# A routed mixture of experts: blocks by rank of count, shared weights, and pairs of small experts

## The chip, the cores and the metric

The kernel runs on one core of a Trainium2 chip. The metric is device time in microseconds. The core's engines are TensorE (PE in the rows, its weight loads PEld), VectorE (DVE), ScalarE (ACT), GpSimd (POOL) and SyncE (SP), which issues most transfers. Each has its own queue and works it in order.

## The reference

Top-k attention, a dense mixture, and a routed mixture of eight experts, one after the other. The change lies in the last.

```python
def _moe_ref(x, w_in, w_out, alpha):          # 2304 tokens, 512 wide, hidden 2048
    h = x @ w_in
    g = np.maximum(h, 0.0) + alpha * np.minimum(h, 0.0)
    return g @ w_out

def _moe2_ref(x, w_skip, w_gate, w1, w2):     # 8 experts, hidden 1024
    do_compute = x @ w_skip > 0
    out = x.copy()
    xc = x[do_compute]
    logits = xc @ w_gate
    e_idx = np.argmax(logits, axis=1)
    ...                                       # gate_w: softmax probability of e_idx
    for e in range(E):
        mask = e_idx == e
        h = np.maximum(xc[mask] @ w1[e], 0.0)
        y[mask] = gate_w[mask, None] * (h @ w2[e])
    out[do_compute] = xc + y
```

All values are 32-bit floats.

## The kernel before

Attention runs batch by batch (four of them), and the dense first mixture of one half batch runs between the attention steps of the next. `main` orders all of it: attention steps stand in a table, other work in queues (`todo`, `rowq`, `late`) that `slot` empties by a budget. The last half batch (320 tokens) has no attention beside it: after `main` a loop calls `slot` until the queues are empty. There `up` (L624) and `down` (L670) stream the first mixture's weights through three tiles `wr`, a megabyte each.

Then `rows` routes each half batch. `logits` (L736) gives gate and skip scores, `row` transposes the tokens and stores them (L755, L765), `route` and `rest` choose an expert on VectorE, `ranks` (L815, L816) counts the tokens of each expert by two products, and `slots` gives each token a place in its expert's list. `scatter` (L839) writes an entry per token (its row in the scratch `x2d`, its row in the output, its weight) into the table `tbl` in DRAM, by an indirect transfer that GpSimd issues. `cnt` holds the counts so far.

The second mixture works by blocks of 128 tokens of one expert. A block fetches its entries and its rows of x by indirect transfers (`xgather`, L1012), transposes and splits them (`xsplit`, L1020 to L1022), multiplies by w1 (`first`, L1030), transposes and splits the hidden rows (`hsplit`, L1038 to L1040), multiplies by w2 (`second`, L1048), adds and scatters (`finish`, L1056, L1059). TensorE multiplies in a fast 32-bit format of fewer bits; to keep the precision, each operand is split into a high part (ScalarE's copy) and a low part (VectorE's difference), and each product is made of three: high by high, low by high, high by low. Weights are split as well: one expert's w1 or w2 comes in four tiles of 128x1024 (`wraw`, L995), and `wsplit` splits each (L1001 on ScalarE, L1002 on VectorE). So `first` and `second` are 24 products of 512 columns each.

There are eleven blocks: one early block, one block per expert, and two extra ones. After three of four batches `pick` chooses the expert with most tokens so far; its first 128 tokens are the early block, whose entries and rows are fetched while the first mixture still runs. Its weights are fetched and split from the 38th `slot` of the last loop on (`TL0`, `TL1`), and then again for its second block. `extras` finds on chip the two experts that get the extra blocks. Each block loads and splits its own weights, so there are 88 tiles. `order_` lists them, `loads` and `splits` work the list. What the eleven blocks do not hold, a loop behind them does (`blocks`), one block per turn, only if the count on chip says so.

Of the kernel before, what the change touches and what calls it, by code (L numbers as in the profile page):

```python
# [18 lines left out]
NX = 2  # L19
# [22 lines left out]
ES = 3  # L42
G1 = 12
G2 = 33
RB = 8
# [4 lines left out]
TL0 = 38  # L50
TL1 = 8
TS = 0.6
TG = 6
# [5 lines left out]
def kernel(  # L59
# [132 lines left out]
    sel = const.tile([128, E], F32, name="sel")  # L192
    nc.vector.memset(sel, 0.0)
    est = const.tile([128, 1], F32, name="est")
    nc.vector.memset(est, -1.0)
# [13 lines left out]
    def defaults():  # L209
        nrd = E * RE // 128 + 1  # L210
        dflt = moe.tile([128, nrd, 4], F32, name="dflt", tag="g", bufs=8)
        nc.gpsimd.memset(dflt, 0.0)
        nc.gpsimd.memset(dflt[:, :, 1:2], 4096.0)
        return nc.sync.dma_start(tbl[0:128 * nrd, :].rearrange("(p r) c -> p r c", p=128), dflt)
# [508 lines left out]
    def rows(b, us, colof, x2t, hook, then):  # L723
# [69 lines left out]
        def rest():  # L793
# [4 lines left out]
            for i, u in enumerate(us):  # L798
                base, step = (b * S + u, SF) if u < SF else (b * S + SB, 1)
                v.tensor_scalar(row[:, i, 1:2], pcol, float(step), float(base), op0=OP.mult, op1=OP.add)  # L800
            v.tensor_scalar(c[:, 1], c[:, 1], 1e-9, None, op0=OP.add)
            v.tensor_scalar(c[:, 6], c[:, 3], -1.0, 1.0, op0=OP.mult, op1=OP.add)
            v.tensor_scalar(c[:, 5], row[:, :, 1], float(E * RE + 128), None, op0=OP.add)
            v.tensor_scalar(row[:, :, 0], row[:, :, 1], float(ZR), None, op0=OP.add)
# [42 lines left out]

        parts = [(lambda: not early[0] and rroom(), None), (0.1, logits)] + [(0, None)] * RD
# [11 lines left out]
    outs, wx = [], []  # L860
    NB = 1 + E + NX

    def wtile(half, odd, ch):
        if odd:
            return mr.tile([128, 2, 1024], F32R, name="w2h", tag="w2h", bufs=8)
        if not half:
            return ml.tile([128, 2, 1024], F32R, name="w1h", tag="w1h", bufs=4)

        if ch % 2 == 0:
            if not wx or ch:  # L870
                wx[:] = [xtile(ch // 2).rearrange("p a n s -> p (a n s)")]
            x = wx[0]
        else:
            x = wx.pop()
        c0 = ch % 2 * 2048
        return x[:, c0:c0 + 2048].rearrange("p (a c) -> p a c", a=2)

    early_ = {}

    def pick():  # L880


        v = nc.vector
        w = const.tile([128, 2, E], F32, name="pw")
        c = const.tile([128, 3], F32, name="pc")
        v.tensor_reduce(c[:, 0:1], cnt, axis=AX.X, op=OP.max)
        v.tensor_scalar(w[:, 0], cnt, c[:, 0:1], None, op0=OP.is_ge)
        v.tensor_tensor(w[:, 0], w[:, 0], e8, op=OP.mult)
        v.tensor_reduce(c[:, 1:2], w[:, 0], axis=AX.X, op=OP.max)
        v.tensor_scalar(sel, e8, c[:, 1:2], None, op0=OP.is_equal)  # L890
        v.tensor_scalar(est, c[:, 1:2], -1.0, float(E), op0=OP.mult, op1=OP.add)
        v.tensor_scalar(c[:, 2:3], est, float(RE), pcol, op0=OP.mult, op1=OP.add)
        v.tensor_scalar(w[:, 1], sel, 128.0, None, op0=OP.mult)
        v.tensor_tensor(cnt, cnt, w[:, 1], op=OP.max)
        ri = const.tile([128, 2], I32, name="pri")
        v.tensor_copy(ri[:, 0:1], c[:, 2:3])
        v.tensor_copy(ri[:, 1:2], est)
        experts[0] = nc.values_load(ri[0:1, 1:2], engines=[mybir.EngineType.SP], min_val=0, max_val=E - 1,
                                    skip_runtime_bounds_check_because="an expert by its making")
        early_["ri"] = ri  # L900

    def early_entries():
        t4 = const.tile([128, 4], F32, name="pt4")
        nc.gpsimd.indirect_dma_start(out=t4, out_offset=None, in_=tbl[0:E * RE + 128, :],
                                     in_offset=bass.IndirectOffsetOnAxis(ap=early_["ri"][:, 0:1], axis=0))
        early_["t4"] = t4

    def early_rows():
        ids = const.tile([128, 2], I32, name="pids")
        nc.vector.tensor_copy(ids, early_["t4"][:, 0:2])  # L910
        early_["ids"] = ids
        x = xtile(0).rearrange("p a n s -> p (a n s)")
        wx[:] = [x]
        early_["xg"] = x[:, 4096:4608].bitcast(F32)
        xgather(ids, early_["xg"])

    def first_rows():


        ta = ml.tile([128, 2, E, 4], F32, name="ta", tag="ta", bufs=1)  # L920
        for h in range(2):
            nc.sync.dma_start(ta[:, h], tbl[0:E * RE, :].rearrange("(e n) c -> n e c", n=RE)[h * 128:(h + 1) * 128])
        return ta

    def first_ids(ta):
        v = nc.vector
        s_ = sel[:, :, None].to_broadcast([128, E, 4])
        v.tensor_tensor(ta[:, 1], ta[:, 1], s_, op=OP.mult)
        ns = ml.tile([128, E], F32, name="ns", tag="ns", bufs=1)
        v.tensor_scalar(ns, sel, -1.0, 1.0, op0=OP.mult, op1=OP.add)  # L930
        v.tensor_tensor(ta[:, 0], ta[:, 0], ns[:, :, None].to_broadcast([128, E, 4]), op=OP.mult)
        v.tensor_tensor(ta[:, 0], ta[:, 0], ta[:, 1], op=OP.add)
        ids = ml.tile([128, E, 2], I32, name="idsa", tag="idsa", bufs=1)
        v.tensor_copy(ids, ta[:, 0, :, 0:2])
        return [(ta[:, 0, e], ids[:, e]) for e in range(E)]

    def count():

        gtj = ml.tile([128, E, 18], F32, name="gtj", tag="gtj", bufs=1)
        nc.vector.tensor_tensor(gtj, j128[:, None, :].to_broadcast([128, E, 18]),  # L940
                                cnt[:, :, None].to_broadcast([128, E, 18]), op=OP.is_lt)
        nx = ml.tile([128, E], F32, name="nx", tag="nx", bufs=1)
        nc.vector.tensor_reduce(nx, gtj, axis=AX.X, op=OP.add)
        nc.vector.tensor_tensor(nx, nx, sel, op=OP.subtract)
        nc.vector.tensor_scalar(nx, nx, 0.0, None, op0=OP.max)
# [4 lines left out]
    def extras(kk, n, skip=1):  # L950

        v = nc.vector
        z = ml.tile([128, 2, NX, E], F32, name="z", tag="z", bufs=1)[:, :, 0:n]
        c = ml.tile([128, 4, NX], F32, name="zc", tag="zc", bufs=1)[:, :, 0:n]
        cb = cum[:, None, :].to_broadcast([128, n, E])
        v.tensor_tensor(z[:, 0], cb, kk[:, :, None].to_broadcast([128, n, E]), op=OP.is_le)
        v.tensor_reduce(c[:, 0], z[:, 0], axis=AX.X, op=OP.add)
        v.tensor_tensor(z[:, 1], z[:, 0], cb, op=OP.mult)
        v.tensor_reduce(c[:, 1], z[:, 1], axis=AX.X, op=OP.max)
        v.tensor_tensor(c[:, 1], kk, c[:, 1], op=OP.subtract)  # L960

        v.tensor_scalar(c[:, 1], c[:, 1], 128.0, 128.0 * skip, op0=OP.mult, op1=OP.add)
        v.tensor_scalar(c[:, 2], c[:, 0], est, 128.0, op0=OP.is_equal, op1=OP.mult)
        v.tensor_tensor(c[:, 1], c[:, 1], c[:, 2], op=OP.add)
        v.tensor_scalar(c[:, 2], c[:, 0], float(E) - 0.5, None, op0=OP.is_lt)
        v.tensor_tensor(c[:, 1], c[:, 1], c[:, 2], op=OP.mult)
        v.tensor_scalar(c[:, 3], c[:, 0], float(RE), pcol, op0=OP.mult, op1=OP.add)
        v.tensor_tensor(c[:, 3], c[:, 3], c[:, 1], op=OP.add)
        ri = ml.tile([128, 2, NX], I32, name="ri", tag="ri", bufs=1)
        v.tensor_copy(ri[:, 0, 0:n], c[:, 3])  # L970
        v.tensor_scalar(ri[:, 1, 0:n], c[:, 0], float(E - 1), None, op0=OP.min)
        return ri

    def extra_rows(ri, k):
        t4 = ml.tile([128, 4], F32, name="t4", tag="t4", bufs=NX)
        nc.gpsimd.indirect_dma_start(out=t4, out_offset=None, in_=tbl[0:E * RE + 128, :],
                                     in_offset=bass.IndirectOffsetOnAxis(ap=ri[:, 0, k:k + 1], axis=0))
        return t4

    def extra_ids(t4):  # L980
        ids = ml.tile([128, 2], I32, name="ids", tag="ids", bufs=NX)
        nc.vector.tensor_copy(ids, t4[:, 0:2])
        return ids

    def expert(ri, k):
        return nc.values_load(ri[0:1, 1, k:k + 1], engines=[mybir.EngineType.SP], min_val=0, max_val=E - 1,
                              skip_runtime_bounds_check_because="at most E - 1 by the minimum taken")

    def wfetch(e, half, ch):

        src, nk = ((w1f, KD), (w2f, KE))[half]
        raw = ml.tile([128, 1024], F32, name="wraw", tag="wraw", bufs=RB)
# [4 lines left out]
        return raw  # L997

    def wsplit(half, odd, ch, raw, eng=None):
        hl = wtile(half, odd, ch)  # L1000
        nc.scalar.activation(hl[:, 0], raw, AF.Copy)  # L1001
        nc.vector.tensor_tensor(hl[:, 1], raw, hl[:, 0].bitcast(F32), op=OP.subtract)  # L1002
        return hl
# [499 lines left out]
```

## Time and profile before

| | us |
|---|---|
| median of three runs (lowest, highest) | 1060.57 (1058.77, 1061.43) |
| the profiled execution | 1059.77 |
| its span | 1058.0 |
| TensorE busy in the span | 922.0 (87%) |
| VectorE busy | 903.6 (85%) |
| ScalarE busy | 685.3 (65%) |
| GpSimd busy | 372.4 (35%) |
| bytes moved | 249.94 MB, 236 GB/s in the mean |

The shares are means over stages with different limits: attention with the first mixture beside it until about 820 us, the first mixture's last half batch alone until 888, and the second mixture from there. What an edit is worth is read from its stage. In the rows, `us` behind a start is the time from the first instruction's start to the last one's end in a merged row; a bracket says how long the engine had been idle and which work ended that. A product of full 32-bit floats appears as two records, of the fast format as one.

### The profile page before, as it was taken

What the parts mean: (1) busy time and instruction counts of PE and PEld (TensorE: products, weight loads), DVE (VectorE), ACT (ScalarE), POOL (GpSimd) and SP (SyncE); (2) the same over time, 40 slices, a digit from 0 to 9 for tenths busy, and PEclk for the clock granted to TensorE, in tenths of its full rate; (3) what the DMA queues carried; (4) which work ended last, traced back from release to release, by engine and by line L of the source; (5) the groups of instructions that cost most, each with busy time, mean ns of one, the idle gap of its engine ahead of it and who ended that gap; (6) DMA issues with size and microseconds to landing.
All of it is one profiled execution on the core that took longest, in us unless ns stands there. A gap on an engine that the chain in (4) does not pass through costs nothing.

```text
span 1058.0 us, 21752 instructions
## 1 busy us (share of the span) xinstructions
PE 922.0 (87%) x7206; PEld 834.9 (79%) x7206; DVE 903.6 (85%) x2943; ACT 685.3 (65%) x1740; POOL 372.4 (35%) x529
## 2 busy tenths in 40 slices
PE   4446578999999989999988999998889898898995
PEld 2334468898999879899988998998889897687884
DVE  5999999998998999899979998998993334798972
ACT  7879867666765776576557667756663443596860
POOL 5865643323421342253123323401421421336220
PEclk9967689998999999999989999999999998899998
DMA  8979886576565667766556777665557898899960
GB/s 239 338 249 255 273 264 216 191 243 188 190 223 205 195 195 236 249 206 221 186 162 218 230 234 239 207 218 174 178 186 269 258 377 325 279 354 398 344 223 16
DMA packets 137387, 249.94 MB, mean 236 GB/s; under 512 B 61166, under 2 KB 93934, under 8 KB 120880
## 3 DMA queue, kind: packets, MB, share of 16 engines
q1 hardware_dynamic: 133568, 243.65, 68.5%
q0 software_dynamic: 2496, 4.50, 1.2%
q8 instruction: 59, 0.97, 0.4%
q14 instruction: 64, 0.52, 0.2%
q10 hardware_dynamic: 1200, 0.30, 0.1%
HBM read 220.00 MB, written 29.71 MB: 236 GB/s over the span
## 4 chain that ended last, share of the span: by engine, by line
PE 53%; DVE 27%; DMA 5%; ACT 4%; issue 3%; POOL 1%; SPq 0%; POOLq 0%; DVEq 0%; ACTq 0%
PE pm L670 18%; PE pm L624 10%; DVE v L457 6%; PE px L549 5%; DVE Ex L490 4%; PE ps L1048 4%; PE pm L1030 4%; PE ps L427 3%; DVE F L460 3%; PE pt L516 3%; DVE ra L637 3%; DVE F L448 3%; DVE m L448 2%; DMA wr<-wout 2%; PE ps L421 1%
## 5 line engine op out<-in xcount | busy, mean ns | idle before, releaser
L624 PE MATMUL pm<-x,wr 128*128 128x256 f32 (+1 forms) x1536 | 247.3, 309 | 18.9 <-DVE ra L637 14.2
L670 PE MATMUL pm<-g,wr 128*128 128x256 f32 (+1 forms) x1536 | 234.7, 303 | 6.1 <-DMA wr<-wout 3.3
L624 PEld LDWEIGHTS pm<-x,wr 128*128 128x128 f32 x1536 | 215.9, 194 | 29.0 <-DVE ra L637 19.1
L670 PEld LDWEIGHTS pm<-g,wr 128*128 128x128 f32 x1536 | 209.0, 189 | 11.8 <-issue 3.6
L457 DVE MAX8 v<-F 128x8 f32<-128x72 f32 (+2 forms) x576 | 214.0, 408 | 0.9
L108 POOL TENSOR_TENSOR g<-ra,g 128x256 fp32r<-128x256 f32 (+1 forms) x128 | 103.3, 815 | 199.5 <-DVE st L495 65.6
L460 DVE MATCH_REPLACE8 F<-v,F 128x72 f32<-128x72 f32 (+1 forms) x432 | 123.4, 292 | 0.0
L432 ACT ACTIVATE sb<-ps 128x288 f32<-128x288 f32 x224 | 80.3, 411 | 65.4 <-PE ps L427 52.9
L490 DVE SCALAR_TENSOR_TENSOR Ex<-sb,v,Ex 128x577 f32<-128x577 f32 x144 | 122.2, 878 | 0.0
L482 ACT ACTIVATE Ex<-sb,st 128x576 f32<-128x576 f32 x144 | 104.7, 775 | 0.1
L643 ACT ACTIVATE g<-ra 128x256 fp32r<-128x256 f32 (+1 forms) x128 | 57.3, 447 | 69.4 <-DVE ra L637 68.7
L637 DVE SCALAR_TENSOR_TENSOR ra<-ra,slope,pm 128x256 f32<-128x256 f32 (+1 forms) x128 | 65.0, 508 | 42.2 <-ACT ra L634 41.7
L528 ACT ACTIVATE PT<-pt 128x512 f32<-128x512 f32 x144 | 86.5, 601 | 22.3 <-PE pt L516 21.8
L108 POOL TENSOR_TENSOR x<-xf,x 128x128 fp32r<-128x128 f32 (+1 forms) x80 | 37.4, 468 | 177.3 <-DVE st L495 107.7
L549 PE MATMUL px<-PT,vt 128*64 128x128 f32 (+1 forms) x1280 | 89.4, 287 | 0.0
L516 PE MATMUL pt<-ident,Ex 128*128 128x128 f32 x576 | 84.1, 279 | 4.9 <-ACT sb L432 4.8
L427 PE MATMUL ps<-kT,qT 64*128 64x288 f32 x576 | 80.0, 350 | 6.7 <-ACT kT L337 2.5
L549 PEld LDWEIGHTS px<-PT,vt 128*64 128x64 f32 x1280 | 70.2, 148 | 9.8 <-issue 2.0
L427 PEld LDWEIGHTS ps<-kT,qT 64*128 64x128 f32 x576 | 61.7, 212 | 20.3 <-issue 9.4
L634 ACT ACTIVATE ra<-pm 128x256 f32<-128x256 f32 (+1 forms) x128 | 52.4, 409 | 39.0 <-PE pm L624 37.1
L516 PEld LDWEIGHTS pt<-ident,Ex 128*128 128x128 f32 x576 | 69.7, 145 | 7.0 <-ACT sb L432 6.5
L448 DVE TENSOR_TENSOR F<-m 128x144 f32<-128x144 f32 (+2 forms) x240 | 66.8, 333 | 0.0
(367 smaller groups left out, 1743.5 us busy)
## 6 DMA issues: line engine op xcount, KB each, us to landing
wr<-win SPq DMA_DIRECT2D x64, 1024.0 KB, 5.1
wr<-wout SPq DMA_DIRECT2D x64, 1024.0 KB, 5.0
wraw<-in_moe_w_dram SPq DMA_DIRECT2D x88, 512.0 KB, 6.3
wr<-in_moe_w_in_dram SPq DMA_DIRECT2D x16, 512.0 KB, 5.8
vt<-in_v_dram SPq DMA_DIRECT2D x32, 256.0 KB, 3.0
win<-cv SPq DMA_DIRECT2D x16, 512.0 KB, 4.5
wr<-in_moe_w_out_dram SPq DMA_DIRECT2D x16, 512.0 KB, 5.3
wout<-cv SPq DMA_DIRECT2D x32, 256.0 KB, 4.2
```

Source lines behind the costliest of these rows:

```text
L108: i = nc.gpsimd.tensor_tensor(o, a, b, op=OP.subtract)
L427: nc.tensor.matmul(self.ps[h, j][:, 0:HALF], lhsT=hd["q"][gp, a, u * 128 - hd["c0"]:(u + 1) * 128 - hd["c0"]], rhs=hd["k"][gp, b_, c0:c0 + ...
L448: gate[0] = nc.vector.tensor_tensor(o[:, n_], a[:, n_, 0:w], a[:, n_, w:2 * w], op=op)
L457: nc.vector.max(v8[:, h, r, :], F[:, h, 0:w])
L460: nc.vector.match_replace(out=F[:, h, 0:w], in_to_replace=v8[:, h, r, :], in_values=F[:, h, 0:w], imm_value=NEG)
L482: nc.scalar.activation(self.Ex[:, h, :], self.sb[:, h, :], AF.Exp, bias=self.st[:, 0, h:h + 1], scale=0.125)
L490: nc.vector.scalar_tensor_tensor(self.Exp[:, cs], self.sbp[:, cs], v8[:, h, 3, 7:8], self.Exp[:, cs], op0=OP.is_ge, op1=OP.mult, accum_out ...
L516: nc.tensor.transpose(pt[:, c * 128:(c + 1) * 128], P[:, c0:c0 + 128], ident)
L549: nc.tensor.matmul(x[h * 64:(h + 1) * 64, 0:n], lhsT=hd["vt"][:, h, c, :], rhs=rhs, start=False, stop=(c == SF - 1))
L624: nc.tensor.matmul(hp[:, 0:n], lhsT=w[:, (f % 2) * 8 + a * 4 + d, :], rhs=x[:, d, c0:c1], start=(i == 0), stop=(i == 3 * KD - 1))
L637: nc.vector.scalar_tensor_tensor(ra, ra, slope[:, f:f + 1], hp[:, 0:n], op0=OP.mult, op1=OP.add)
L670: nc.tensor.matmul(op_[:, 0:n], lhsT=w[:, 2 * f + a, :], rhs=g[(hf + ch) * 8 + f, sg][:, gg, 0:n], start=(i == 0), stop=(i == ni - 1))
```

## The change

It replaces the eleven blocks by nine. `pick` ranks all experts by their count after three batches (`rank`; ties by number). The three first ranks have two blocks each, the fourth one block, and the four last share two blocks: 64 rows each, two experts to a block (`BLOCKS`; a pair is rank and first row in the list). An expert's weights are loaded and split once and serve both of its blocks. The pairs' weights are not split: `product` multiplies them as plain 32-bit floats, once instead of three times, on 64 of the array's columns for each of the two experts. `NEED` lists in which order the halves (0 is w1, 1 is w2) of each rank's weights are loaded, and into which of four places: `wc` (0), the two x tiles (1), and two groups of tiles `wd` (2 and 3). So there are 64 loads, of which 32 are split.

Block 0 and block 1 are both early: ranks 0 and 1, 128 rows each. Block 0's first product stands on both sides of the rank products of the last routing. The counting of leftover blocks (`caps`, `count`) stands behind block 1. The weight loads begin at the second `slot` of the last loop. The rank's numbers go to SyncE by eight register loads. Entries of every block are fetched by an indirect transfer of its own. A block's row numbers are stored as integers, so no conversion is needed when they are read.

```diff
-G1 = 12
-G2 = 33
+G1 = 8
+G2 = 20
+G3 = 44
-TL0 = 38
-TL1 = 8
+TL0 = 2
+TL1 = 6
+TW = 16
+RAW = 4
+BLOCKS = [((0, 0), (0, 64)), ((1, 0), (1, 64)), ((0, 128), (0, 192)), ((1, 128), (1, 192)),
+          ((2, 0), (2, 64)), ((2, 128), (2, 192)), ((4, 0), (5, 0)), ((3, 0), (3, 64)), ((6, 0), (7, 0))]
+NEED = [((0, 0), 0), ((1, 0), 1), ((0, 1), 2), ((1, 1), 3), ((2, 0), 0), ((2, 1), 1), ((3, 0), 0), ((4, 0), 2),
+        ((5, 0), 2), ((3, 1), 1), ((4, 1), 3), ((5, 1), 3), ((6, 0), 2), ((7, 0), 2), ((6, 1), 3), ((7, 1), 3)]
...
+        if b == B - 1 and us[-1] == SF and mid is not None:
+            parts = [(rroom, None), (0.1, logits), (0, None), (0.1, route)]
+            for i in range(nu):
+                parts += [(rroom, None), (0.45, lambda i=i: row(i)), (0, None)]
+            return parts + [(0.0, mid[0]), (rroom, None), (0.1, ranks), (0, None), (0.0, mid[1]),
+                            (0, None), (0.0, hook)]
...
     def pick():
+        v.scalar_tensor_tensor(key, cnt, 16.0, e8, op0=OP.mult, op1=OP.add)
+        v.tensor_tensor(w, key[:, None, :].to_broadcast([128, E, E]), key[:, :, None].to_broadcast([128, E, E]),
+                        op=OP.is_gt)
+        v.tensor_reduce(rank, w, axis=AX.X, op=OP.add)
...
+    def product(o, st, w, ks, n, c0, first, last):
+        whole, raw, i = len(w) == 1, not isinstance(w[0][0], tuple), 0
+        terms = [(0, 0)] if raw else order
+        tot = len(ks) * len(terms)
+        for k in ks:
+            for (a, b_) in terms:
+                for g, W in enumerate(w):
+                    gs = slice(0, 128) if whole else slice(g * 64, (g + 1) * 64)
+                    lhs = st[:, k * 128:(k + 1) * 128][:, gs] if raw else st[:, a, k * 128:(k + 1) * 128][:, gs]
+                    rhs = W[k] if raw else W[k][b_]
+                    nc.tensor.matmul(o[gs], lhsT=lhs, rhs=rhs[:, c0:c0 + n], start=first and i == 0,
+                                     stop=last and i == tot - 1)
+                i += 1
...
+        if gone == 1:
+            perms()
+        if gone == G1:
+            ent[0], ent[1] = entries(0), entries(1)
+        if gone == G2:
+            xgather(ent[0], xgs[0], x2d[0:ZR + NT - S, :])
+        if gone == G3:
+            x_(0)
...
+        if gone >= TL0 and gone % TL1 == 0 and nload[0] < 16 and len(pend) < RB:
+            when[nload[0]] = gone
+            load()
...
+    for kb in range(2, NB):
+        ent[kb] = entries(kb)
+        if 2 < kb < 7:
+            xg_(kb - 1)
+    h_(0)
+    split(4)
+    load(4)
+    f_(1)
+    split(4)
+    load(4)
+    s_(0)
+    h_(1)
+    o_(0)
+    s_(1, 0)
+    x_(2)
+    s_(1, 1)
+    f_(2)
+    x_(3)
+    h_(2)
+    split(4)
+    load(4)
+    o_(1)
+    caps()
+    count()
...
+    for kb in range(3, NB + 1):
+        if kb < NB:
+            f_(kb)
+        if kb + 1 < NB:
+            x_(kb + 1)
+        if kb in (3, 5):
+            split(4)
+        s_(kb - 1)
+        if kb == 6:
+            split(4)
+        load({3: 12, 4: 8, 6: 8, 7: 8}.get(kb, 0))
+        if kb < NB:
+            h_(kb)
+        o_(kb - 1)
+        if kb + 3 < NB:
+            xg_(kb + 3)
```

Here `x_`, `f_`, `h_`, `s_` and `o_` are a block's `xsplit`, two halves of `first`, `hsplit`, `second` and `finish`; `mid` holds the two halves of `f_(0)`; `xg_` fetches a block's rows.

TensorE around the last routing, before (`pm` and `ps` are PSUM tiles, `x2t` the first mixture's result, `oh` the chosen experts, `hrow` the hidden rows):

```order
L736 MATMUL ps<-wg,x2t 128x9 x8
L736 MATMUL ps<-wg,x2t 64x9 x4
L755 MATMUL ps<-ident,x2t 128x128 x8
L815 MATMUL ps<-oh,tri 128x24
L816 MATMUL ps<-oh,ones 128x24
L755 MATMUL ps<-ident,x2t 64x128 x4
L1020 MATMUL ps<-ident,x 128x128 x4
L1030 MATMUL pm<-w1h,xs 128x512 x24
L1038 MATMUL pt<-ident,hrow 128x128 x8
L1048 MATMUL ps<-x,hs 128x512 x24
```

and with the change:

```order
L760 MATMUL ps<-ident,x2t 128x128 x8
L760 MATMUL ps<-ident,x2t 64x128 x4
L1018 MATMUL pm<-wc_12229,xs 128x512 x3
...
L821 MATMUL ps<-oh,tri 128x24
L822 MATMUL ps<-oh,ones 128x24
...
L1018 MATMUL pm<-wc_12232,xs 128x512 x3
L1030 MATMUL pt<-ident,hrow 128x128 x8
L1018 MATMUL pm<-x,xs 128x512 x24
L1018 MATMUL ps<-wd,hs 128x512 x24
L1030 MATMUL pt<-ident,hrow 128x128 x8
L1018 MATMUL ps<-wd,hs 128x512 x12
L998 MATMUL px<-ident,xg 128x128 x4
```

The transposes of blocks 0 and 1 have moved into the first mixture, twelve products of block 0 stand on each side of the rank products, and the first product of block 1 stands ahead of the second of block 0.

GpSimd behind the last scatter of table entries, with the change (`bt` holds a block's entries; before, three row gathers of L1012 stood here):

```order
L845 DMA tbl<-row,slot 21888x4
L935 DMA bt_12964<-tbl,pri 128x4
L935 DMA bt_12966<-tbl,pri 128x4
L991 DMA xg<-x2d,bt_12964 128x512
L935 DMA bt_12970<-tbl,pri 128x4
L991 DMA xg<-x2d,bt_12966 128x512
```

and VectorE at that time:

```order
L839 TENSOR_TENSOR cnt<-tot,e_row 128x8
L1036 TENSOR_TENSOR hs<-pt,hs 128x512 x2
L988 TENSOR_TENSOR wd<-wraw,wd 128x1024 x8
L1036 TENSOR_TENSOR hs<-pt,hs 128x512 x2
L1043 SCALAR_TENSOR_TENSOR orow<-ps,bt_12332,x 128x512
```

Each block's rows now wait for an entry fetch of its own, and eight splits stand in a row on VectorE, where the count of leftovers stood.

TensorE at the end of the kernel, with the change (64x512 are the pairs' products, on half of the columns):

```order
L1018 MATMUL pm<-wd,xs 64x512 x16
L998 MATMUL px<-ident,xg 128x128 x4
L1018 MATMUL ps<-x,hs 128x512 x24
...
L1018 MATMUL ps<-wd,hs 64x512 x16
L1030 MATMUL pt<-ident,hrow 128x128 x8
L1018 MATMUL pm<-wd,xs 64x512 x16
L1018 MATMUL ps<-x,hs 128x512 x24
L1030 MATMUL pt<-ident,hrow 128x128 x8
L1018 MATMUL ps<-wd,hs 64x512 x16
```

Four groups of 16 products stand where groups of 24 stood.

## Rows read from the trace of the kernel before

**Rows 1.** Stretches: engines' busy us and instructions, granted clock, share of the DMA engines, GB/s.

```profile
core 0: us, PE busy (x) PEld busy (x) DVE busy (x) ACT busy (x) POOL busy (x), PEclk, DMA share, GB/s
888.40:896.00 7.60, 6.61 (x45) 5.64 (x44) 5.19 (x33) 4.12 (x10) 0.76 (x1) 0.70 0.48 139
896.00:901.00 5.00, 2.07 (x4) 1.16 (x4) 4.35 (x26) 2.82 (x3) 2.32 (x5) 0.50 0.94 335
...
916.00:960.00 44.00, 43.30 (x208) 35.60 (x209) 42.24 (x45) 39.78 (x51) 21.33 (x8) 1.00 0.99 367
...
972.00:1038.00 66.00, 66.00 (x315) 54.62 (x315) 53.45 (x57) 45.78 (x59) 13.42 (x14) 0.99 0.72 270
```

**Rows 2.** Timeline, TensorE at the last routing, then VectorE: start, us, what.

```profile
888.36 2.53 PE L736 MATMUL ps<-wg,x2t 128*128 128x9 f32 x24
890.82 1.45 PE L755 MATMUL ps<-ident,x2t 128*128 128x128 f32 x8
...
893.46 1.04 PE L755 MATMUL ps<-ident,x2t 128*64 128x128 f32 x4
...
896.04 2.07 PE L1030 MATMUL pm<-w1h,xs 128*128 128x512 f32 x4 [0.69 <-ACT xs L1021]
901.17 6.70 PE L1030 MATMUL pm<-w1h,xs 128*128 128x512 f32 x20 [3.05 <-DVE xs L1022]
...
895.07 0.31 DVE L940 TENSOR_TENSOR gtj<-j,cnt 128x144 f32<-128x144 f32 x1
```

**Rows 3.** Timeline, TensorE in the steady part of the second mixture.

```profile
995.80 0.60 PE L1020 MATMUL ps<-ident,xg 128*128 128x128 f32 x4
996.15 5.73 PE L1048 MATMUL ps<-x,hs 128*128 128x512 f32 x24
...
1002.52 5.84 PE L1030 MATMUL pm<-w1h,xs 128*128 128x512 f32 x24
1008.20 0.60 PE L1020 MATMUL ps<-ident,xg 128*128 128x128 f32 x4
```

**Rows 4.** Chain that ended last, behind the last product: start, us, what.

```profile
1045.86 0.76 DVE orow L1056
1046.66 0.51 POOLq L1415
1047.16 0.71 POOL out_dram L1059
```

**Rows 5.** Timeline, TensorE in the last block.

```profile
1038.31 1.03 PE L1038 MATMUL pt<-ident,hrow 128*128 128x128 f32 x8
...
1040.32 5.51 PE L1048 MATMUL ps<-x,hs 128*128 128x512 f32 x23 [0.22 <-DVE hs L1040]
```

**Rows 6.** Chain, a full-width 32-bit product; then timelines cut at 801.0 and 801.2 us.

```profile
800.65 0.22 PE px L545 x2
...
800.80 0.44 PE L549 MATMUL px<-PT,vt 128*64 128x128 f32 x4
...
800.80 0.66 PE L549 MATMUL px<-PT,vt 128*64 128x128 f32 x8
```

**Rows 7.** Timeline, GpSimd's transfers, VectorE's splits, TensorE's wait; last, median issue to landing.

```profile
906.51 0.98 POOL L1012 DMA_INDIRECT xg<-x2d,idsa  x1 [7.75 <-DVE idsa L934]
...
918.86 4.36 POOL L1012 DMA_INDIRECT xg<-x2d,idsa  x1 [0.30 <-issue]
...
917.76 4.62 DVE L1002 TENSOR_TENSOR w2h<-wraw,w2h 128x1024 fp32r<-128x1024 f32 x4
...
969.50 0.75 PE L1020 MATMUL ps<-ident,xg 128*128 128x128 f32 x4 [2.85 <-DMA xg<-x2d,idsa]
...
xg<-x2d,idsa POOLq DMA_INDIRECT x8, 7.4
```

**Rows 8.** Waits from 820 to 889 us: total us, times, longest.

```profile
PE pm L670 <- DMA wr<-wout: 3.3, 3, 1.3
...
PE pm L670 <- ACT x L1001: 1.5, 1, 1.5
```

**Rows 9.** Timeline, GpSimd's low half of the queries, then the products that read it.

```profile
746.92 0.73 POOL L108 TENSOR_TENSOR qT<-raw__11057,qT 128x256 fp32r<-128x256 f32 x1
...
750.25 0.80 PE L427 MATMUL ps<-kT,qT 64*128 64x288 f32 x7
```

More of the change, by code (lines that the diff above doesn't have):

```diff
@@ L18 @@
 NEG = -3.0e38
-NX = 2
 BMIN = 4.3
@@ L721, with rows @@
     scats = []
-    def rows(b, us, colof, x2t, hook, then):
+    def rows(b, us, colof, x2t, hook, then, mid=None):
         nu = len(us)
@@ L859 @@
     w2f = w2.rearrange("e f d -> (e f) d")
[L860 to L876, printed above, removed]
+    outs = []
+    order = [(0, 0), (1, 0), (0, 1)]
     early_ = {}
@@ L892, in pick @@
[L892 to L899, printed above, removed]
@@ L917, in first_rows @@
[L917 to L935, printed above, removed]
+        wk = rp.tile([128, 5, 4, E], F32, name="rt", tag="rt", bufs=1).rearrange("p a b e -> p (a b) e")
@@ L974, in extra_rows @@
[L974 to L987, printed above, removed]
@@ L1090, in until, with parts_of @@
-    def until(*last):
-        if last in order_:
-            splits(4 * order_.index(last) + 4 - nsplit[0])
+        return nc.gpsimd.indirect_dma_start(out=out, out_offset=bass.IndirectOffsetOnAxis(
+            ap=t4.bitcast(I32)[:, 1:2], axis=0), in_=orow, in_offset=None, bounds_check=NT - 1, oob_is_err=False)
+    def parts_of(views, half):
+        out_ = []
+        for v in views:
+            pair = v.dtype == F32R
+            for a in range(1 + half):
+                c = slice(a * DM, (a + 1) * DM) if half else slice(0, FE)
+                out_.append((v[:, 0, c], v[:, 1, c]) if pair else v[:, c])
+        return out_
@@ new lines, in split, with weights, is_raw @@
+    def split(n):
+        for _ in range(n):
+            r, half, ch, at, raw = pend.pop(0)
+            hl = mr.tile([128, 2, 1024], F32R, name="wd", tag=f"wd{at}{ch}", bufs=1) if at > 1 else group[at][ch]
+            wsplit(hl, raw)
+            W.setdefault((r, half), []).append(hl)
+    def weights(k, half):
+        rs = sorted({r for r, o in BLOCKS[k]}, key=[r for r, o in BLOCKS[k]].index)
+        return [parts_of(W[r, half], half) for r in rs]
+    def is_raw(k):
+        return BLOCKS[k][0][0] >= RAW
@@ new lines, in s_, with o_, xg_ @@
+    def s_(k, half=None):
+        if half != 1:
+            yps[k] = htile()
+        fs = range(KE) if half is None else range(half * KE // 2, (half + 1) * KE // 2)
+        second(hss[k], weights(k, 1), yps[k], fs)
+    def o_(k):
+        s = finish(yps[k], ent[k], xgs[k])
+        for o in outs:
+            tc.declare_no_dep(s.ins, o.ins, reason="other rows")
+        outs.append(s)
+    def xg_(k):
+        xgs[k] = mr.tile([128, DM], F32, name="xg", tag="xg", bufs=4)
+        xgather(ent[k], xgs[k])
@@ L1330 @@
     ml = ml_ctx.enter_context(tc.tile_pool(name="ml", bufs=1, reuse_waits="tile"))
[L1331 removed]
+    group[0] = [ml.tile([128, 2, 1024], F32R, name=f"wc{i}", bufs=1) for i in range(4)]
+    t, two_ = place(0)
+    group[1].extend(two_)
+    xgs[0] = t[:, 4096:4608].bitcast(F32)
+    gone, when = 0, {}
     while todo or late or rowq:
         slot(TS)
[L1334 to L1343 removed]
@@ L1358, in one @@
-    def one(i):
-        hr = mr.tile([128, FE], F32, name="hrow", tag="hrow", bufs=1)
-        for j in range(2):
-            first(xss[i], W[0, i], hr, j)
-        return hr
-    def two(i, hr):
-        hss[i] = mr.tile([128, 2, FE], F32R, name="hs", tag="hs", bufs=1)
-        for j in range(2):
-            hsplit(hr, hss[i], j)
-    def end(i):
-        def ahead():
-            if 0 < i and i + 4 < NB:
-                xgs[i + 4] = xgather(rows_[i + 4][1])
-        s = finish(yps[i], *rows_[i], xgs[i], ahead)
-        for o in outs:
-            tc.declare_no_dep(s.ins, o.ins, reason="other rows")
-        outs.append(s)
@@ L1380 @@
[L1380 to L1412 removed]
+        gone += 1
@@ new lines @@
+        if gone == 1:
[6 more added lines that the diff above has]
+            x_(0)
+        if len(group[1]) == 2 and len(ups) == len(work) and gone > G2:
+            t, two_ = place(1)
+            group[1].extend(two_)
+            xgs[1] = t[:, 4096:4608].bitcast(F32)
+            xgather(ent[1], xgs[1], x2d[0:ZR + NT - S, :])
+            when["x"] = gone
```

401 lines of the change are left out of this document (200 added, 201 removed).

## Prediction

> **What bounds the kernel now.** I read the stretches of busy time first, then TensorE's order of time, then the other engines where TensorE waits. The change leaves attention and nearly all of the first mixture alone; it lives after 888.4 us, where the first mixture's last product ends, and in the 60 us before, where weights are fetched ahead.
>
> Three things bound that tail. First the routing: from 888.4 to about 901 TensorE does little, and what it does runs at half clock, 0.70 and then 0.50 granted [rows 1]. The logits, the row transposes, then block 0's transposes and its first four products stand there, and then TensorE sits 3.05 us until VectorE has the low half of block 0's rows [rows 2]. VectorE was late because the count of leftover blocks, which began at 895.07, stood ahead of it in its order [rows 2]. Block 0's first product ends at 907.9 (901.17 + 6.70). Then VectorE's weight splits: from 916 to 960 it is busy 42.24 us of 44, TensorE 43.30. From 972 on TensorE alone is full (66.00 of 66) and VectorE has slack [rows 1]. There one block costs one pitch: from 995.80 to 1008.20 are 12.4 us: 0.35 for the row transposes (x), 6.4 for the second product (s, 5.6) with the transposes of the hidden rows (h, 0.8), and 5.7 for the first product (f) [rows 3]. Eleven blocks at that pitch are the tail.
>
> **The sum.** The profiled execution took 1059.77 us, of which 1058.0 are span; the median of the runs is 0.8 more. Between the last product (1045.86) and the span's end lie 12.1 us [rows 4], which the change doesn't touch. So I add up TensorE's path from 888.4 to the last product, 157.5 us now.
>
> *Routing.* Logits 2.5, row transposes 1.4 and about 1.0 [rows 2]. Then half of block 0's first product, since its rows and weights are ready beforehand: 12 products. The clock is half here; four took 2.07 [rows 2], so twelve take about 5.2; at full clock they would take 2.9. The two rank products (about 1.0, as the last transposes) and the other half (2.9, half of f) follow. Together 14.0 (2.5 + 2.4 + 5.2 + 1.0 + 2.9): block 0's first product ends at 902.4, 5.5 us before the present one. The routing work on VectorE now runs beside these products. The leftover count moves behind block 1, where VectorE waits for TensorE anyway; without that cover it would cost up to the 5 us between 895.07 and VectorE's part of block 0's rows.
>
> *Blocks 0 to 2.* h0 1.3 (0.8 and, as an estimate, 0.5 of the open copy that follows f0), f1 5.7, s0 5.6. Then h1 and s1 stand directly behind each other, so the copy out and the low half lie open, as at the end of the kernel now: 1038.31 to 1040.32, 2.0 [rows 5]. s1 with block 2's transposes inside 6.0, f2 5.7, x3 and h2 1.7. That is 28.0, and a wait for block 2's rows of 3 (below): 31.0, to 933.4.
>
> *Three ordinary pitches* (f3 to h5): 37.2, to 970.6. VectorE has at most four splits (4.62 [rows 7]) in a pitch where it had eight, so it no longer presses: the 88 split tiles become 32.
>
> *The unsplit pairs.* Blocks 6 and 8 multiply plain 32-bit weights, two experts of 64 rows side by side, 16 products of 512 columns in each half. No such shape is in the trace, but its small form is: the values product, 64 columns wide, 128 columns moving, alternating between the two halves of the array. A full-width one of 128 columns takes 0.22 in two records. The narrow ones run two at a time: four records end after 0.44, eight after 0.66, so four more records, a pair of products, cost 0.22, as one full-width product does [rows 6]. Four times the columns make 0.88 a pair, eight pairs 7.0. Bounds: below, nothing under 24 split products (5.5); above, no overlap, 14.1. I take 7.0 because the narrow rows are the same kind of instruction; their start-up weighs less at 512 columns. So f6 7.0, x7, s5 and h6 6.7, f7 5.7, x8, s6 and h7 8.2, f8 7.0, s7 5.6, h8 with its open copy 2.0, s8 7.0: 49.2, to 1019.8.
>
> That is 26.1 before the present last product: 1059.8 - 26.1 = **1033.7**, with the median's 0.8 about **1034**. Where it comes from: two blocks fewer (2 x 12.4), about 5.5 at the routing, 2.9 from the present wait for rows at 969.5 [rows 7]; less 4 x 1.4 for the pairs, the 3 us wait and the open copies.
>
> *Edits that I set to nothing.* Weight loads fall from 88 to 64. In the tail the last ones bind most: eight for s8 can start only when s6 has freed their place, and have h7, f8, s7, h8, 15.4 us, for 4.2 MB; at the 367 GB/s of the busy stretch [rows 1] that is 11.4, so they just hide. In the first mixture the fetches start at the beginning instead of the second half. Now TensorE loses 3.3 + 1.5 there waiting for weights and x [rows 8]. The same bytes spread evenly could remove these 4.8, or the eight register loads ahead of a first-mixture weight load, four splits beside the activations, and the fetches between could bring as much again. Zero, with 4.8 either way. The ranking puts some 20 memsets on GpSimd ahead of the low half of the next queries, which is done at 747.65 and wanted at 750.25 [rows 9]: 2.6 us of cover. The low half itself takes 0.73 for 256 columns; a memset of one column I estimate at 0.1 to 0.3, 20 of them at 2 to 6. Zero, with 3 as the end. Nine small VectorE operations for the row numbers stand ahead of an activation in the first mixture: under 1.
>
> *Block 2's rows.* Now 13 us pass from the rank products (893.46) to the first row gather (906.51) [rows 2, 7]; after the change the ranks end at about 899, so that gather would be issued at 912, and 3 to 4 later because entries are fetched one block at a time by GpSimd. Landed 7.4 later [rows 7], it is 923; TensorE wants it at 920 (902.4 + 1.3 + 5.7 + 5.6 + 2.0 + half of s1). Hence the 3. A gather's issue takes 0.98 when VectorE isn't splitting, and 4.36 when four splits run (917.76 for 4.62; the gather of 918.86 ends nearly a microsecond behind them) [rows 7]. The change puts eight splits behind each other just there. If each of the two entry fetches lost a group, the wait would be 9; if none did, 0.
>
> The Trainium skill ("SBUF — State Buffer", section "SBUF: two separate sides") says that GpSimd can't write the descriptors of its own transfers while VectorE holds the port that they share, so that such a transfer looks blocked. Here the rows agree: 4.36 against 0.98. By that rule, with both groups unbroken, the wait would be the 9, and the time 1040.
>
> **Rivals.** *Late rows and weights.* The split groups hold up GpSimd's fetches (+6) and the first mixture loses 3 more to weights or queries: 1043. For it speaks the stall that the kernel has already, 2.85 us until a gather lands [rows 7]; against it, the fetches are all issued early, and between the groups VectorE has to wait for ScalarE's copies.
>
> *The pairs do not overlap at 512 columns.* Then each of four halves takes 14.1: +28.4, 1062, no change within measure. The rows of the narrow product speak against it.
>
> *Leftover blocks: slower.* The small experts have one place of 64 rows each, where they had 128. Ranks are taken from three of four batches. One row over in one expert, and the loop behind the kernel runs once, with nothing beside it: entry and row fetch 14.8, two groups of splits 9.3, a block 12.4, about 36: 1070, slower. It decides at row 65 (129 for the fourth, 257 for the first three). By the reference's own arithmetic for these inputs the counts are 217, 176, 150, 68, 46, 39, 35 and 37 in order of rank: the nearest is 18 rows away. The change does what it says: TensorE's order shows the same weight tile in f0 and f2.
>
> **How the numbers follow.** Forecast 0.70, late rows and weights 0.20, pairs without overlap 0.06, leftovers 0.04. The forecast's own ends: no half clock (-2.3), no row wait (-3), no waits in the first mixture (-4.8) give 1024; row wait 9 (+6), first mixture +4.8, queries +3 give 1048. The range is 1022 to 1048, which leaves out the last two and a little beside. About 0.3% (3.2 us) is what can be told from no change: the first two cases are faster (0.90), the third mostly the same (0.05), the rest slower (0.05).
>
> **What would show it.** Right: nine blocks; f0 beginning some 5 us after the logits' start; 16 products on 64 columns in about 7 us with a start-to-start of 0.44 per record pair; the last product near 1020; VectorE well under full after 930. Wrong: 14 us for such a group; TensorE idle over 5 us at block 2's transposes, with GpSimd's fetch drawn out beside eight splits; a first mixture that ends after 893; a loop body that runs.

## The result, and the profile after

The change makes the kernel faster. On the chip that timed both, its median was 1030.87 us (four runs, 1027.34 to 1036.04) against 1061.0 before: ratio 0.972, 95% interval 0.968 to 0.977. Timed again later it was 1034.19 (five runs, 1031.67 to 1035.19), ratio 0.973 (0.971 to 0.976). The forecast was 1034.

The profiled execution took 1030.26 us, 29.5 less than that of before. TensorE's timeline shows where its second mixture stands:

```profile
816.34 1.95 PE L741 MATMUL ps<-wg,x2t 128*128 128x9 f32 x16
...
891.71 2.53 PE L741 MATMUL ps<-wg,x2t 128*128 128x9 f32 x24
894.17 1.53 PE L760 MATMUL ps<-ident,x2t 128*128 128x128 f32 x12
895.46 3.04 PE L1018 MATMUL pm<-wc,xs 128*128 128x512 f32 x12
898.34 0.29 PE L821 MATMUL ps<-oh,tri 128*128 128x24 f32 x2
...
898.70 3.04 PE L1018 MATMUL pm<-wc,xs 128*128 128x512 f32 x12
901.57 0.60 PE L1030 MATMUL pt<-ident,hrow 128*128 128x128 f32 x4
...
920.35 0.66 PE L998 MATMUL px<-ident,xg 128*128 128x128 f32 x4 [1.55 <-DMA xg<-x2d,bt]
...
936.70 0.60 PE L998 MATMUL px<-ident,xg 128*128 128x128 f32 x4
...
949.12 0.60 PE L998 MATMUL px<-ident,xg 128*128 128x128 f32 x4
...
968.48 7.09 PE L1018 MATMUL pm<-wd,xs 128*64 128x512 f32 x32
...
1010.63 7.09 PE L1018 MATMUL ps<-wd,hs 128*64 128x512 f32 x32 [0.25 <-ACT hs L1033]
```

The first row starts the next to last logits, the second the last ones. Block 0's first product is done at 901.57, where the transposes of its hidden rows begin. Against [rows 2] the 3.05 us wait for VectorE is gone. A steady pitch is 949.12 - 936.70 = 12.4 as in [rows 3]. The pairs' 16 products take 7.09 us (32 records). The last product ends at 1017.7, and 10.8 us later the span. TensorE's waits from 810 to 895 (total us, times, longest) begin with a group of three, 1.85, 3.24 and 1.50 us for the activation `ra`, that the kernel before did not have. The wait for `fl`, the certificate's flag, it had too, at 2.0:

```profile
PE pm L629 <- DVE ra L642: 6.6, 3, 3.2
PE pt L1372 <- DVE fl L1370: 2.8, 1, 2.8
PE pm L675 <- DMA wr<-wout: 0.7, 1, 0.7
```

The stretches show the clock and VectorE's share (columns as in [rows 1]; the first row is the stage between the two logits):

```profile
816.34:891.71 75.37, 65.13 (x427) 63.57 (x424) 25.77 (x67) 25.66 (x50) 20.18 (x26) 0.95 0.82 317
...
847.00:867.00 20.00, 15.26 (x93) 14.72 (x92) 7.10 (x10) 9.04 (x16) 6.16 (x8) 0.91 0.73 278
...
892.00:901.00 9.00, 9.00 (x60) 7.97 (x61) 3.23 (x29) 2.85 (x8) 0.55 (x1) 1.00 0.51 152
916.00:960.00 44.00, 42.22 (x201) 34.33 (x202) 21.72 (x41) 16.85 (x25) 12.06 (x17) 1.00 0.73 272
```

From 916 to 960 VectorE is busy 21.72 us of 44 where it had 42.24 [rows 1], and in the routing the granted clock is 1.00 where it was 0.70 and 0.50. The same stage in the kernel before:

```profile
819.61:888.36 68.75, 61.29 (x418) 59.66 (x415) 21.88 (x55) 23.73 (x47) 18.23 (x24) 1.00 0.92 339
```

Step by step, in the profiled executions:

| step | forecast | measured |
|---|---|---|
| start of the next to last logits (before: 819.61) | 0 | -3.3 |
| from there to the last logits (before: 68.75) | 0, within 4.8 | 75.37, so +6.6 |
| last logits to the end of block 0's first product | 14.0 | 9.9 |
| blocks 0 to 2, to block 3's first product (930.53) | 31.0 | 29.0 |
| three pitches, to 968.48 | 37.2 | 38.0 |
| pairs and what stands between, to 1017.7 | 49.2 | 49.2 |
| behind the last product | 12.1 | 10.8 |

The first line is not the change's: in thirteen profiles of this kernel and its variants those logits start between 815.7 and 820.4. From the last logits to the last product the tail was 5.4 us shorter than summed (126.0 against 131.4), and the first mixture 6.6 longer than assumed. The two nearly cancel.

### The profile page after: what moved, and what is told of

Read it like the earlier page. It is cut to its first block, busy times and chain, and to the rows that moved or that the text cites. A ratio compares the mean times of both kernels' runs of the same rounds, so it can differ in the third digit from the quotient of the medians.

```text
span 1028.5 us, 21422 instructions
## 1 busy us (share of the span) xinstructions
PE 896.7 (87%) x7118; PEld 800.5 (78%) x7118; DVE 830.0 (81%) x2864; ACT 626.8 (61%) x1674; POOL 349.8 (34%) x548
## 4 chain that ended last, share of the span: by engine, by line
PE 57%; DVE 26%; ACT 4%; DMA 3%; issue 2%; POOL 1%; SPq 0%; POOLq 0%; ACTq 0%; DVEq 0%
PE pm L675 19%; PE pm L629 10%; DVE v L462 6%; PE px L554 5%; PE pm L1018 4%; PE ps L1018 4%; DVE Ex L495 4%; PE pt L521 3%; PE ps L432 3%; DVE F L465 3%; DVE ra L642 3%; DVE F L453 3%; DVE m L453 2%; PE ps L426 1%; PE px L550 1%
## 5 line engine op out<-in xcount | busy, mean ns | idle before, releaser
L648 ACT ACTIVATE g<-ra 128x256 fp32r<-128x256 f32 (+1 forms) x128 | 57.3, 448 | 74.6 <-DVE ra L642 72.3
```

## Experiments

A time given without a number of runs is that of a single execution.

**What made the first mixture longer.** I read the mechanism from the timelines of ScalarE, VectorE and TensorE in the changed kernel, around the first of the three waits (start, us, what, idle before and what ended it):

```profile
840.65 0.44 ACT L639 ACTIVATE ra<-pm 128x320 f32<-128x320 f32 x1 [1.76 <-PE pm L629]
...
841.35 1.05 ACT L987 ACTIVATE wc<-wraw 128x1024 fp32r<-128x1024 f32 x1
...
842.43 1.23 DVE L988 TENSOR_TENSOR wc<-wraw,wc 128x1024 fp32r<-128x1024 f32 x1 [2.96 <-ACT wc L987]
843.57 0.54 DVE L642 SCALAR_TENSOR_TENSOR ra<-ra,slope,pm 128x320 f32<-128x320 f32 x1
...
844.16 3.78 PE L629 MATMUL pm<-x,wr 128*128 128x320 f32 x24 [1.85 <-DVE ra L642]
```

ScalarE's part of the activation `ra` is done at 841.09. VectorE could finish it then, but a split stands ahead in its order and waits until 842.43 for ScalarE's copy of the weights; the activation comes at 843.57, and only then is the PSUM bank free for TensorE. The rivals: the early fetches fill the DMA engines, or the clock did it. Two edits remove the stall in different ways and leave the fetches where they are:

```diff
-        if pend and n < 8 and when[n] + TW <= gone and (n < 4 or n - 4 < len(group[1])):
+        if pend and n < 8 and when[n] + TW <= gone and len(ups) == len(work) and gone % 6 == 4 and \
+                (n < 4 or n - 4 < len(group[1])):
```

> The weight fetches stay as early as in the changed kernel; the eight splits of expert 0's and 1's first weights are all put behind the last activation of the first mixture's up products. Theory (the stage from the last half batch's queue work to the logits grew from 68.7 to 75.4 us because four VectorE splits, each waiting for its ScalarE copy, stand ahead of the activation that frees TensorE's PSUM bank): TensorE's three waits for that activation, 1.85, 3.24 and 1.50, fall to under 0.7 in sum, and the stage comes to 68 to 71. Rival (the early fetches fill the DMA engines, or the half clock of 825 and 852 made the stage longer): the stage stays at 73 or more, and TensorE's wait shows on the weight tiles.

The three waits are gone, the stage is 68.87 us, the time 1025.06.

```diff
     def wsplit(hl, raw, lag=0):
         nc.scalar.activation(hl[:, 0], raw, AF.Copy)
+        def low():
+            nc.vector.tensor_tensor(hl[:, 1], raw, hl[:, 0].bitcast(F32), op=OP.subtract)
+        if lag:
+            late.append((lag, low))
+        else:
+            low()
...
-            split(1)
+            split(1, 4)
```

> The eight splits stay where they are, but the VectorE half of each is issued four slots behind its ScalarE half, so that VectorE no longer stands still for the copy. Theory (it is the standing still, about 1.1 us of copy plus the copy's own place in ScalarE's order, that hurts, more than the 1.23 us of the split): the 6.6 us of waits fall to 1 to 2.5, the stage to 69.5 to 72. Rival (VectorE's 1.23 us themselves are too much there): waits of 4 or more remain, the stage at 73 or more.

The stage is 68.67, the time 1026.18; one wait of 1.2 is left. VectorE's timeline shows why: the splits stay among the activations, at the same 1.2 us each, but with at most 0.40 of standing still ahead:

```profile
845.97 1.22 DVE L990 TENSOR_TENSOR wc<-wraw,wc 128x1024 fp32r<-128x1024 f32 x1
847.30 0.55 DVE L642 SCALAR_TENSOR_TENSOR ra<-ra,slope,pm 128x320 f32<-128x320 f32 x1
...
850.00 1.23 DVE L990 TENSOR_TENSOR wc<-wraw,wc 128x1024 fp32r<-128x1024 f32 x1 [0.40 <-ACT wc L987]
```

So it is the waiting in order, not VectorE's work and not the fetches: the first version keeps the fetches where they are, the second keeps the splits among the activations as well. Nor is it the clock: with the late splits its mean over the stage is 0.95, as in the changed kernel. Both versions and the changed kernel were timed again:

> The split in two steps again, now timed: 1024 to 1027, that is 4 to 6 us less than the changed kernel's median of 1030.9.

> The late splits again, now timed: 1024 to 1027; within 1.5 us of the split in two steps if it is the activation's wait that both remove.

> The changed kernel itself, timed again, to set its distance to the two versions with later splits (1026.2 and 1027.3). Theory (their gain is the 6.6 us of waits on the activation, which this kernel has): median 1029 to 1034, the three waits of 1.85, 3.24 and 1.50 there again, stage 75 to 78. Rival (the first profile was an unlucky one): median 1025 to 1028, the stage at 70 to 73.

Two steps: 1026.24 (six runs), ratio 0.967 (0.965 to 0.970). Late splits: 1027.28 (five), 0.968 (0.966 to 0.970). The change again: 1034.19, 0.973 (0.971 to 0.976), with the same three waits and the stage at 78.2. Each ratio is against the kernel before on the same chip. The intervals of the first and the last don't meet: by them the split in two steps beats both kernels, the changed one by 0.6% (0.9674 / 0.9732). The changed kernel's first timing, 0.968 to 0.977, overlaps with it, so the size of this gain is less sure than the waits that it removes.

**A second stall moved, not removed.** With the late splits, the product that forms the certificate's flag (TensorE waits 2.78 for it at 824.99) went behind block 2:

```diff
-    pf = ptile()
-    nc.tensor.matmul(pf[0:1, 0:1], lhsT=fl, rhs=ones[:, 0:1], start=True, stop=True)
...
     count()
+    pf = ptile()
+    nc.tensor.matmul(pf[0:1, 0:1], lhsT=fl, rhs=ones[:, 0:1], start=True, stop=True)
```

> Two edits on the changed kernel: the eight early splits behind the last activation of the up products, and the one-column product with the certificate's flag (TensorE waits 2.78 us for VectorE at 824.99, in both kernels) moved to the count of leftover blocks. Expected: no wait on the activation (6.6) and none on the flag (2.8): the stage from the next to last logits to the last logits 65.5 to 67 instead of 75.4, the time 1021 to 1024. If the flag's wait only uncovers another (the activations behind it are late too), the stage is 68 to 69 and the time 1024 to 1027.

1025.71 (six runs), ratio 0.969 (0.966 to 0.972), stage 68.15: 0.7 less than with the late splits alone, where 2.8 was hoped for. A wait for `ra` of 2.4 takes its place, and the interval of the late splits alone (0.966 to 0.970) covers this one's ratio. (The flag's wait is 2.78 in the changed kernel; in the kernel before it was 2.03, not the same.) TensorE waits again where the product went:

```profile
925.19 0.19 PE L1433 MATMUL pt<-ones,fl 128*1 128x1 f32 x2 [1.15 <-DVE hs L1036]
```

**Is the cut product a cover?** The prediction counted on the first half of block 0's product to cover VectorE's routing. But VectorE has its choice at 895.8 and the ranks come at 898.34. So the product was made whole, behind the ranks:

```diff
     def mid0():
-        f_(0, (0,))
         return []
     def mid1():
-        f_(0, (1,))
+        f_(0)
         return []
```

> Block 0's first product is no longer cut in two: the rank products come first, the whole of it behind them. In the changed kernel VectorE has the choice ready at 895.8 and the rank products run at 898.34, behind the first half. Theory A (the ranks start the chain that fetches block 2's rows, so they wait 2.5 us for nothing): ranks at about 896.0, TensorE idle there for 0.5 at most, block 0's first product done within 0.7 of where it was, block 2's rows 2.5 us earlier, TensorE's wait for them 1.55 to 0 to 0.3: the tail is 1 to 1.5 us shorter, 124.5 to 125.2 from the logits to the last product instead of 126.0. Rival B (the prediction's view: the first half is the cover of VectorE's routing): TensorE idles up to 3 us ahead of the ranks and the tail is longer, 127.5 to 129.

> The same two edits, and the last rank products ahead of block 0's first product, which is whole again. By theory A of that experiment (the row fetch of block 2 starts 2.5 us earlier and its wait, 0 to 2.4 in the profiles so far, is always 0) it is 0.5 to 1.5 us faster than the same kernel without it; by rival B 1.5 to 3 slower.

Alone, the tail took 125.9 against 126.0, with the transposes at half clock (1036.18 in all, with a first mixture of 77.7). The like to compare it with are the two profiles of the split in two steps, at the same half clock and with no wait for rows either: 126.0 and 126.4. On top of the late splits and the moved flag it took 128.4 against 128.1, and the median 1028.92 (ratio 0.971, 0.969 to 0.973) against 1025.71 (0.969, 0.966 to 0.972). Both theories fail. Alone, TensorE doesn't idle ahead of the ranks; on top of the other edits it idles 0.68, not 3:

```profile
892.51 0.37 PE L821 MATMUL ps<-oh,tri 128*128 128x24 f32 x2 [0.68 <-DVE rc L802]
```

And the earlier scatter does not land earlier. In that kernel the last one is issued 9.7 us behind the logits (887.84) and the first entry fetch waits for it until 16.1:

```profile
897.52 0.91 POOL L845 DMA_INDIRECT tbl<-row,slot  x1 [0.21 <-issue]
...
903.90 1.08 POOL L935 DMA_INDIRECT bt<-tbl,pri  x1 [5.47 <-DMA tbl<-row,slot]
```

In the changed kernel the scatter comes at 11.3 and the fetch at 14.7. The medians differ by 3.2 us, just outside rival B's 1.5 to 3, but the tails differ by 0.3 and the intervals overlap: whether the order of the ranks costs anything is not shown.

**What the scatter waits for.** Two weight fetches of half a megabyte are issued just ahead of it. In the version with two steps, one early fetch every five slots instead of six (`TL1 = 5`) puts all of them ahead of the logits:

> The split in two steps, and all sixteen early weight fetches issued before the last logits (one every five slots instead of six); in every profile of the changed kernel's kind two of them, 1 MB, are issued 7.4 to 8.5 us behind the start of the last logits, just ahead of the scatter of the routing entries, and the first entry fetch starts 14.6 to 16.1 us behind the logits wherever the ranks stand. Theory (the scatter lands late because its packets stand behind those two fetches and the row writes on the DMA engines): the first entry fetch starts at 12 to 13.5 behind the logits, and TensorE has no wait for block 2's rows (0 to 2.7 so far). Rival (what lands late is the scatter's own latency): 14.6 or later. In the first mixture the tighter fetches could cost 0 to 2 of waits for its own weights. Time 1023 to 1026.

The entry fetch starts at 13.6 and waits 1.35 for the scatter; block 2's rows are in time:

```profile
906.32 1.47 POOL L935 DMA_INDIRECT bt<-tbl,pri  x1 [1.35 <-DMA tbl<-row,slot]
```

The wait of 1.35 alone says little: three profiles with those two fetches still in the way have it too, because half clock in the routing delays their scatter to 12.9 behind the logits (their fetch starts at 15.1 to 15.2). The start is what speaks for the theory, though 13.6 is just outside its 13.5: the scatter is issued at 11.3 here, and in the seven other profiles that issue it there the fetch starts at 14.7 to 15.5. For the whole it is worth nothing, since the same two steps without it had no wait for the rows either. The price is in the first mixture, whose own weights come late, 2.0 and 1.4:

```profile
PE pm L675 <- DMA wr<-wout: 2.0, 1, 2.0
PE pm L629 <- DMA wr<-win: 1.4, 2, 0.9
```

The stage is 72.3, the median 1029.46 (ratio 0.968, 0.966 to 0.971) against 1026.24 (0.967, 0.965 to 0.970): no gain.

**The leftover count, back to its old place** (`caps` and `count` ahead of block 0's `h_`, its hidden rows):

> The count of leftover blocks goes back to where it stood: directly behind the last routing, ahead of block 0's hidden rows on VectorE. It is some fifteen small operations, about 4 us as VectorE shows them in the changed kernel. Theory A (block 1's first product, 5.8 us on TensorE, now stands between block 0's transposes and its second product, so it covers most of this): block 0's second product begins 0 to 1.5 us later, the tail is 126 to 128 instead of 126.0 (or 124.3 to 126 where block 2's rows are in time). Rival B (the count was what held block 0 in the kernel before, and does so again, as the prediction said of the case without cover): 3 to 5 us later, the tail at 129 to 131.

VectorE's count runs from 907.9 to 911.2, and the hidden rows' low halves follow at 911.21 instead of at once. TensorE doesn't notice: the second product starts 5.66 behind block 1's first one, as in the changed kernel (5.67):

```profile
910.48 5.82 PE L1018 MATMUL pm<-x,xs 128*128 128x512 f32 x24
916.14 5.64 PE L1018 MATMUL ps<-wd,hs 128*128 128x512 f32 x24
```

The tail is 126.5, theory A (1036.63 in all, with a first mixture of 77.6); the two profiles of the split in two steps, at the same half clock, have 126.0 and 126.4. So the move is worth at most some 0.5 here, with block 1's first product as the cover, and it is not what removed the 3.05 us of before. What is left as the reason is that block 0's rows are now transposed and split before the routing; that alone was not undone.

**The pairs' order.** One expert's products first, then the other's (in `product`, the loop over `w` outermost):

> Blocks 6 and 8 now issue all sixteen half-products' worth of one expert on its 64 columns, then all of the other's, instead of alternating. Theory (two products on different halves of the array run at the same time only if they stand next to each other): a half of a paired block, 7.05 us for its 16 products in the changed kernel, becomes about 14.1; four halves make +28, so the last product moves from 1017.7 to about 1046 and the time is near 1059. Rival (each 64-column product simply costs half of a full-width one, whatever stands beside it): 7.05 stays and the time stays near 1031.

```profile
970.93 8.97 PE L1019 MATMUL pm<-wd,xs 128*64 128x512 f32 x32
...
992.92 12.29 PE L1019 MATMUL ps<-wd,hs 128*64 128x512 f32 x32
```

The two kinds of halves take 8.97 and 12.29 instead of 7.09, and the time is 1046.62. Neither number was expected. In the second kind of half, the records of one expert start 0.43 us apart, so 32 in series would take about 14; the other expert's first four records run beside the former's last four, which saves 4 x 0.43 = 1.7. In the first kind the expert changes three times, since each 512 hidden columns are done for both: 3 x 1.7 = 5.1, and 14.1 - 5.1 = 9.0. This is an estimate made after the fact. It says that products on different halves of the array overlap when they stand within about two products of each other; alternating gets all of it.

**A fetch beside splits.** Four splits were moved behind block 2's output rows, beside GpSimd's fetch of block 6's rows:

> Four VectorE splits move from 941.8 to behind block 2's output rows, so that GpSimd's fetch of block 6's rows (issued at 949.85 in the changed kernel, 1.00 us, with the DMA engines full and VectorE idle) now stands beside four splits in a row. Theory A (the prediction's reading: a fetch can't get past VectorE while a split runs): its issue takes 4 us or more. Theory B (beside a split a fetch waits for a gap between two instructions of VectorE, as the 1.5 to 2.0 us of the changed kernel's fetches at 906 to 913): 1.2 to 2.2 us. Theory C (VectorE does not matter): 1.0. The time as a whole should not move by more than its spread, since the fetched rows are wanted some 25 us later.

```profile
950.27 1.98 POOL L991 DMA_INDIRECT xg<-x2d,bt  x1 [0.30 <-issue]
...
947.90 4.62 DVE L988 TENSOR_TENSOR x<-wraw,x 128x1024 fp32r<-128x1024 f32 x4
```

1.98 instead of 1.00, with the DMA engines at a share of 1.03: theory B. The time was 1032.23.

## Why the prediction was right, point by point

*The routing* was to end 14.0 us behind the logits and took 9.9. Nearly all of the difference is the clock: logits, transposes, 12 products, ranks and 12 products took 2.5, 1.3, 2.9, 0.4 and 2.9, at a granted 1.00. The sum took half clock from [rows 1], and 1.0 for the ranks. In four of the twelve later profiles (the split in two steps both times, the ranks first alone, the count early) the granted clock there is 0.85 and the term 11.4 to 11.5, so it swings by 1.6 us from profile to profile. The wait for VectorE went, as said; what the sum put beside it, the cut product and the moved count, was not what removed it (above).

*Blocks 0 to 2*: the wait for block 2's rows was taken at 3 and measured 1.55. In the other twelve profiles it is 0 nine times, the changed kernel's own second profile among them, and 1.6 to 2.7 three times. (893.46, which the prediction calls the rank products, is the row of the transposes behind them.) The bounds 0 and 9 came from reading a fetch of 4.36 beside a split [rows 7] as a fetch that cannot get past VectorE. This reading fell: in thirteen profiles of the changed kernel and its variants no entry or row fetch took over 1.98, eight splits or not. The Trainium skill ("SBUF — State Buffer", section "SBUF: two separate sides") says that whichever of VectorE and GpSimd starts first holds the shared port for its whole instruction. The changed kernel and its variants agree with that: beside splits of 1.2 us each a fetch takes at most about 1 us longer. The step from one instruction to a whole group was the prediction's own, from the 4.36, and the 1040 that came of it is out. What made fetches take 4.4 to 4.9 in the kernel before was not tried and stays open.

*Three pitches* held (38.0 against 37.2), and VectorE has slack as said.

*The pairs* held in size and reason: 7.09 against 7.0, by the narrow rows [rows 6]. The rival without overlap is out, and the order is what does it. The last weights hid: the last second product waits 0.25, for ScalarE.

*Leftover blocks*: no loop body ran. *The queries* kept their time: the memsets took 1.1 us (744.69 to 745.81), inside the 2.6 of cover.

*The first mixture* is the step that failed. It was set to zero with 4.8 either way and measured +6.6. The good side came: waits for weights and for a split fell from 3.3 + 0.6 + 1.5 to 0.9. But the 4.8 on the other side was only the good side turned round. Nothing was worked out for the four splits beside the activations; they stood among the things that "could bring as much again". Their price was the order: a split that waits for ScalarE, with the activation behind it and TensorE behind that, three times, 6.6 us. A hint lay in [rows 8]: the 1.5 read there as a wait for x is put down to L1001, ScalarE's half of a weight split that writes into an x tile.

That the waits and the longer stage are both 6.6 is chance. In the stage TensorE is idle 2.8 us more than before (10.24 against 7.46: the three waits 6.6 more, the flag 0.8 more, weights and split 4.5 less) and busy 3.8 us more (65.13 against 61.29). Of the 3.8, 0.7 are the transposes of blocks 0 and 1, which the prediction took out of the tail and added nowhere; the rest, some 3, is by estimate the granted clock, 0.95 where it was 1.00.

One of the prediction's signs of being wrong, a first mixture that ends after 893, did not show in the first profile, which started 3.3 early: its last logits begin at 891.71, those of the five other profiles with the three waits at 895.6 to 897.9.

*The sum* adds up, but its list of where the 26.1 comes from does not: 24.8 + 5.5 + 2.9 less 5.6 and 3 is 24.6, before the open copies are taken off.

So the time came out within 4 us of the forecast in part by luck: a shorter tail and a longer first mixture, each off by more than the total is. The mechanisms of the tail (fewer blocks, the pairs, VectorE's slack) held.

## What to carry over

When an instruction that depends on another engine is put among the work of a pipeline, price its wait, not its length: 1.2 us of VectorE's work cost up to 3.2 us of TensorE, because what it waited for stood at the end of another queue. Issue the two halves of such a step apart, by a few slots. And take a cover out once to see that it covers something: of the edits at the routing, the cut product and the moved count gained nothing that these profiles show.

## What had not been expected of the hardware

A stall can cost twice. In all six profiles with the three waits of 1.85, 3.24 and 1.50, the granted clock from 847 to 867 us is 0.74 to 0.91: TensorE is at 1.2 GHz for a part of it, from within 1.5 us of the end of a wait. In the seven with later splits, and in the kernel before, it is 1.00. The stages fall apart in the same way: 75.4 to 78.2 us against 68.2 to 69.2, or 72.3 where weights came late.

Not every stall does it. From the next to last to the last logits of all fourteen profiles, the clock fell behind the wait of 3.24 in six of six, behind the flag's 2.78 in ten of eleven, behind a wait of 2.4 in two of two, behind the only one of 1.98, behind 1.85 in three of six, and not behind the flag's 2.03 in the kernel before; behind those of 1.50 and less it never fell. So the kernels without the three waits pay as well: with the late splits the clock is at half for 7 us behind the flag's wait, and over the whole stage its mean is 0.95, as in the changed kernel's first profile (0.91 in its second). This stretch is of the changed kernel run again, where 24 products took 5.32 us instead of 3.75:

```profile
849.10:852.50 3.40, 3.40 (x16) 3.40 (x15) 0.00 (x0) 0.76 (x2) 0.87 (x1) 0.57 0.99 406
```

And this is the version with two steps, timed:

```profile
849.10:863.00 13.90, 13.61 (x94) 13.37 (x93) 7.18 (x9) 7.40 (x15) 7.11 (x8) 1.00 1.02 409
```
